# One load for wq, a pair of K tiles at the start, mirrored regions and zeros at the end, in a decode attention kernel bound by its load queue

## Chip, cores and metric

One Trainium2 chip, one core of it. The metric is the device time of one execution in microseconds (us). All runs that are compared here are of the state "fast". The profile's span leaves out some 1.9 us of each execution (381.3 us of 383.2).

## The reference

Two branches share one token x of 1024 numbers, and a sigmoid gate g mixes them:

```python
q = (x @ wq)                                   # 32 heads of 128
k, v = k_cache, v_cache                        # 4 head groups, 65536 keys each; 8 query heads share one
p = softmax(q k^T * 128**-0.5)
a = (p v) @ wo
b = (z1 * (w_sp * layernorm(z2) + b_sp)) @ w_out     # z = gelu(x @ w_in), halves z1 and z2
out = g * a + (1 - g) * b
```

162.0 MB must be read: K and V are 67.1 MB each, wq and wo 8.4 each, w_in 7.3, w_out 3.7.

## The kernel before

One buffer `kv` of five regions of 4 MB each takes every large load. A load may start once the region is no longer read. A group's K or V is four tiles of 4 MB, mostly loaded as two pairs of 8 MB. The instructions of each engine run in the order of the program.

```python
kv = big.tile([P, NKV * CT * P], BF16, name="kv")      # 5 regions of 4 MB

def load(src, shape, at):                              # at: region, may be a fraction
    ...
    ins = nc.sync.dma_start(out=v, in_=src)            # all of them on SP's queue (SPq)

win = load(win_view, (KC, F), 3)                       # regions 3 and 4
wq_t = [load(wq_view[:, i * KH:(i + 1) * KH, :], (KH, HD), 1 - i) for i in range(2)]
...                                                    # first branch, then q = x @ wq

def k_tile(g, j, kn):
    for v in range(VC):                                # four quarters
        nc.vector.transpose(...)                       # DVE, in place: L385
        while late:
            nc.vector.reduce_max(**late.pop())         # maximum of the tile before: L387
        ...                                            # 8 matmuls of 512 columns, PE: L392
    nc.scalar.copy(out=sct[g, j][:], in_=s_ps[:])
    late.append(...)

def stats(g): ...      # maximum over the group, exp on ACT, four transposes of p on DVE (L428)
def v_tile(g, j, vt): ...                              # 32 matmuls on PE: L438

build_w(0)
for j in range(NT):                                    # K of group 0: four loads
    k_tile(0, j, load_kv(A_k_cache, 0, j, (2, 1, 0, 3)[j])[0])
    if j == 1:
        build_w(1)
project(load(w_out, (FC, D), 4), FC, uT, 0, first=True)    # (view of w_out cut)
stats(0)
for g in range(1, G):
    for h in range(2):
        kn = load_kv(A_k_cache, g, 2 * h, 1 - h, 2)    # K: regions 1,2 and then 0,1
        for i in ((0, 1), (1, 0))[h]:
            k_tile(g, 2 * h + i, kn[i])
        ...
        vn = load_kv(A_v_cache, g - 1, 2 * h, 3, 2)    # V: regions 3,4
        v_tile(g - 1, 2 * h, vn[0])
        if h == 1:
            stats(g)
        v_tile(g - 1, 2 * h + 1, vn[1])
    head_out(g - 1)
...                                                    # last V, head_out, then wo in pieces of 16,8,4,2,1,1
```

## Time and profile before

| | before |
|---|---|
| time, median of 3 runs | 383.21 us (383.08 to 383.3) |
| span in the profile | 381.3 us |
| load queue's share of the DMA engines | 98.7% |
| DVE, PE busy | 57%, 60% |

From the page of the kernel before: the busy time of the engines, the share of the DMA engines and the GB/s in 40 slices of 9.5 us, and the load queue (packets, MB, share of 16 engines' time).

```profile
span 381.3 us, 2579 instructions
PE 230.5 (60%) x1372; PEld 56.4 (15%) x796; DVE 218.4 (57%) x211; ACT 39.6 (10%) x55; POOL 4.4 (1%) x10
...
DMA  9999999999999999999999999999999999999995
GB/s 385 440 433 416 423 429 440 440 485 429 407 412 419 440 442 433 433 433 440 440 428 440 440 440 440 435 434 399 419 440 435 426 440 427 426 414 433 437 412 225
...
q1 hardware_dynamic: 4180, 162.01, 98.7%
```

The queue is never short of work: only the last slice is below 9. The other engines matter where they make a load late, and after the last load.

Whether a load is late is read from the timeline of SP, which issues the loads. The columns are the start, the length of the issue itself, and what is loaded. The kernel before, 60 to 160 us:

```profile
71.80 0.33 SPq L167 DMA_DIRECT2D kv<-in_A_k_cache_dram  x1
95.92 0.33 SPq L167 DMA_DIRECT2D kv<-in_A_v_cache_dram  x1
119.11 0.33 SPq L167 DMA_DIRECT2D kv<-in_A_k_cache_dram  x1
137.00 0.33 SPq L167 DMA_DIRECT2D kv<-in_A_v_cache_dram  x1
```

The four are K of group 1 (first half), V of group 0 (first half), K of group 1 (second half) and V of group 0 (second half). The packet records in the trace tell when the queue reaches each. The packets of a load end with 16 packets of 4 bytes, as many as there are DMA engines; the first of these shows when an engine is through with the load before and turns to the next one: at 85.3, 104.7, 124.1 and 143.4 us. I call the time from the issue to that moment the *lead*: 13.5, 8.7, 4.9 and 6.4 us. In the rest of the loop it is 3.9 to 5.7 us.

What makes those loads come when they do is the work on DVE and PE. Timeline of the kernel before, some groups of instructions (start, busy us, engine, line, operation; in brackets the idle time before it and what ended it):

```profile
70.52 2.30 DVE L385 STREAM_TRANSPOSE kv<-kv 128x2048 int32<-128x2048 int32 x1
...
94.16 1.71 PE L479 MATMUL out_ps<-kv,uT 128*32 128x256 bf16 x56
...
106.90 11.09 DVE L385 STREAM_TRANSPOSE kv<-kv 128x2048 int32<-128x2048 int32 x5 [1.30 <-DMA kv<-in_A_k_cache_dram]
109.31 11.50 PE L392 MATMUL s_ps<-kv,wt 128*128 128x512 bf16 x40 [11.20 <-DVE kv L385]
```

DVE starts tile 2 of group 0 at 70.5 us without having waited. All K work of group 0 is done at 94.2, where PE goes on to w_out. At 106.9 DVE is waiting when K of group 1 lands. Its first tile is used up at 119.1, and that frees the region which the K load at 119.11 needs.

The moved bytes around that load, in stretches of 2 us (start:end, length, busy us and count of PE, PEld, DVE, ACT, POOL, then granted clock, DMA share, GB/s). A packet is counted where it starts, so single stretches jump:

```profile
122.00:124.00 2.00, 0.35 (x2) 0.10 (x1) 2.00 (x2) 0.00 (x0) 0.00 (x0) 1.00 0.38 164
124.00:126.00 2.00, 1.70 (x9) 0.29 (x3) 2.00 (x2) 0.00 (x0) 0.00 (x0) 1.00 1.21 524
126.00:128.00 2.00, 1.74 (x8) 0.38 (x4) 2.00 (x2) 0.00 (x0) 0.00 (x0) 1.00 1.06 459
128.00:130.00 2.00, 1.96 (x10) 0.40 (x5) 0.77 (x4) 0.03 (x1) 0.00 (x0) 1.00 1.14 492
```

And the end of the kernel before, from the landing of the last piece of wo:

```profile
378.86 0.41 PE L479 MATMUL out_ps<-kv,oa 128*32 128x256 bf16 x4 [0.25 <-DMA kv<-in_A_wo_dram]
...
379.31 0.37 ACT L522 CAST out_sb<-out_ps 128x256 bf16<-128x256 f32 x1 [45.27 <-PE out_ps L479]
379.71 0.33 SPq L525 DMA_DIRECT2D out_dram<-out_sb  x1
```

### The profile page before, as it was taken

The page shows a single profiled execution, that of the slowest core. Times are in us where ns is not written, and L with a number is a line of the kernel's source. Part 1 is how long each engine was busy: PE and PEld are TensorE (multiplying, and loading weights), DVE is VectorE, ACT ScalarE, POOL GpSimd, SP SyncE. Part 2 cuts the span into 40 slices and gives each one's busy share as a digit, 9 for nine tenths or more (in the row PEclk, how much of TensorE's full clock was granted, in tenths as well). Part 3 has the DMA queues.
Part 4 walks back from the last instruction along what each step waited for, and adds up shares of the span by engine and source line. Part 5 has one row for each costly group of instructions (what it writes and reads, how often), then busy time and mean ns, then how long its engine had stood idle before and what let it go on. Part 6 is the DMA issues. An engine that isn't in the chain of part 4 may idle for free.

```text
span 381.3 us, 2579 instructions
## 1 busy us (share of the span) xinstructions
PE 230.5 (60%) x1372; PEld 56.4 (15%) x796; DVE 218.4 (57%) x211; ACT 39.6 (10%) x55; POOL 4.4 (1%) x10
## 2 busy tenths in 40 slices
PE   0064467678157934796397638872976196849355
PEld 0011011112011200121011101120111011212123
DVE  4133487996687506966977059669960488560040
ACT  1001001111601100114011001040100010500000
POOL 4000000000000000000000000000000000000000
PEclk9995659998859995989589958895989579969766
DMA  9999999999999999999999999999999999999995
GB/s 385 440 433 416 423 429 440 440 485 429 407 412 419 440 442 433 433 433 440 440 428 440 440 440 440 435 434 399 419 440 435 426 440 427 426 414 433 437 412 225
DMA packets 4231, 162.17 MB, mean 425 GB/s; under 512 B 504, under 2 KB 508, under 8 KB 892
## 3 DMA queue, kind: packets, MB, share of 16 engines
q1 hardware_dynamic: 4180, 162.01, 98.7%
q8 instruction: 8, 0.13, 0.1%
q14 instruction: 3, 0.02, 0.0%
q10 hardware_dynamic: 40, 0.01, 0.0%
HBM read 162.01 MB, written 0.00 MB: 425 GB/s over the span
## 4 chain that ended last, share of the span: by engine, by line
DMA 57%; PE 24%; DVE 14%; ACT 2%; issue 1%; SPq 1%; DVEq 0%; ACTq 0%
DMA kv<-in_A_k_cache_dram 42%; PE s_ps L392 20%; DMA kv<-in_A_wo_dram 8%; DVE kv L385 8%; DMA kv<-in_A_v_cache_dram 7%; PE o_ps L438 3%; DVE pt L428 2%; DVE o_sb L452 1%; DVE mx L387 1%; ACT sc L403 1%; ACT sc L425 1%; SPq L167 1%; DVE rowt L448 1%; PE om_ps L458 0%; DVE osum L468 0%
## 5 line engine op out<-in xcount | busy, mean ns | idle before, releaser
L392 PE MATMUL s_ps<-kv,wt 128*128 128x512 bf16 x512 | 140.3, 432 | 83.8 <-DVE kv L385 83.8
L385 DVE STREAM_TRANSPOSE kv<-kv 128x2048 int32<-128x2048 int32 x64 | 142.7, 2280 | 56.3 <-DMA kv<-in_A_k_cache_dram 56.3
L438 PE MATMUL o_ps<-kv,pt 128*64 128x512 bf16 x512 | 61.8, 400 | 7.5 <-DMA kv<-in_A_v_cache_dram 7.5
L392 PEld LDWEIGHTS <-wt 128*128 128x128 bf16 x256 | 27.3, 107 | 198.1 <-issue 138.0
L403 ACT CAST sc<-s_ps 128x1024 bf16<-128x1024 f32 x16 | 16.2, 1013 | 250.0 <-PE s_ps L392 250.0
L438 PEld LDWEIGHTS <-pt 128*64 128x64 bf16 x256 | 16.1, 115 | 50.6 <-issue 48.1
L428 DVE STREAM_TRANSPOSE pt<-sc 128x1024 bf16<-128x1024 bf16 x16 | 18.6, 1217 | 6.8 <-ACT sc L425 6.8
L387 DVE TENSOR_REDUCE mx<-sc 128x1 f32<-128x1024 bf16 x12 | 14.5, 1209 | 9.3 <-ACT sc L403 9.3
L425 ACT ACTIVATE sc<-sc,nb 128x1024 bf16<-128x1024 bf16 x16 | 18.2, 1136 | 12.2 <-DVE nb L421 12.2
L448 DVE TENSOR_TENSOR rowt<-o_ps,own 128x1024 f32<-128x1024 f32 x4 | 4.8, 1194 | 24.9 <-PE o_ps L438 24.9
L458 PE MATMUL om_ps<-o_sb,hsel 128*32 128x128 f32 x8 | 2.5, 422 | 19.7 <-DVE o_sb L452 19.7
L407 DVE TENSOR_REDUCE mx<-sc 128x1 f32<-128x1024 bf16 x4 | 4.9, 1220 | 14.4 <-ACT sc L403 14.4
L278 PE MATMUL q_ps<-kv,xT 128*32 128x512 bf16 x64 | 7.2, 630 | 3.7 <-DMA kv<-in_A_wq_dram 3.7
L479 PE MATMUL out_ps<-kv,oa 128*32 128x256 bf16 x128 | 6.7, 368 | 3.6 <-DMA kv<-in_A_wo_dram 2.1
L234 PE MATMUL xb_ps<-xg,spread 8*128 8x256 bf16 x1 | 0.4, 367 | 13.2 <-DMA xg<-in_gate_w_dram 13.2
L452 DVE TENSOR_REDUCE o_sb<-rowt 128x128 f32<-128x1024 f32 x4 | 7.5, 1872 | 0.1
L345 DVE TENSOR_TENSOR rowt<-q_ps,own_b 128x512 f32<-128x512 f32 x2 | 1.3, 685 | 8.8 <-PE q_ps L278 8.8
L278 PE MATMUL z_ps<-kv,xT 128*32 128x448 bf16 x64 | 6.0, 570 | 0.0
L479 PEld LDWEIGHTS <-oa 128*32 128x32 bf16 x128 | 4.4, 124 | 6.0 <-issue 3.2
L522 ACT CAST out_sb<-out_ps 128x256 bf16<-128x256 f32 x1 | 0.4, 372 | 45.3 <-PE out_ps L479 45.3
L238 DVE TENSOR_TENSOR xm<-xb_ps,sel_i 128x128 f32<-128x128 f32 x2 | 0.5, 286 | 8.0 <-PE xb_ps L234 8.0
L278 PEld LDWEIGHTS <-xT 128*32 128x32 bf16 x64 | 2.7, 141 | 11.9 <-issue 11.9
(88 smaller groups left out, 55.5 us busy)
## 6 DMA issues: line engine op xcount, KB each, us to landing
kv<-in_A_k_cache_dram SPq DMA_DIRECT2D x4, 4096.0 KB, 46.9
kv<-in_A_wq_dram SPq DMA_DIRECT2D x2, 4096.0 KB, 33.0
kv<-in_A_v_cache_dram SPq DMA_DIRECT2D x2, 4096.0 KB
kv<-in_B_w_in_dram SPq DMA_DIRECT2D x1, 7168.0 KB
kv<-in_A_wo_dram SPq DMA_DIRECT2D x1, 4096.0 KB
kv<-in_B_w_out_dram SPq DMA_DIRECT2D x1, 3584.0 KB
kv<-in_A_wo_dram SPq DMA_DIRECT2D x1, 2048.0 KB
kv<-in_A_wo_dram SPq DMA_DIRECT2D x1, 1024.0 KB, 30.6
```

The lines of the kernel that those rows point to most:

```text
L278: ins = nc.tensor.matmul(ps[t * B:(t + 1) * B, k * HN:k * HN + n], lhsT=xT[:, i * KH + c:i * KH + c + 1].to_broadcast([P, B]), rhs=w[:, c, ...
L385: nc.vector.transpose(out=kb[:, v * n:(v + 1) * n], in_=kb[:, v * n:(v + 1) * n])
L387: nc.vector.reduce_max(**late.pop())
L392: ins = nc.tensor.matmul(s_ps[:, k * HN:(k + 1) * HN], lhsT=wt[g % 2][:, v, b].rearrange("p a v h -> p (a v h)"), rhs=kx[:, b // 2, b % 2, ...
L403: nc.scalar.copy(out=sct[g, j][:], in_=s_ps[:])
L407: nc.vector.reduce_max(**late.pop())
L425: nc.scalar.activation(out=sct[g, j][:], in_=sct[g, j][:], func=ACT.Exp, scale=SCALE, bias=nb[:, 0:1], accum_out=lss[g][:, j:j + 1])
L428: nc.vector.transpose(out=ptt[g, j][:].rearrange("p c x -> p (c x)"), in_=sct[g, j][:])
L438: ins = nc.tensor.matmul(o_ps[g][hs, e, :], lhsT=ptt[g, j][:, 2 * u:2 * u + 2, :].rearrange("p c x -> p (c x)"), rhs=vx[:, 2 * u + e], sta ...
L448: nc.vector.tensor_tensor(out=om8, in0=o_ps[g][:].rearrange("p e (v d) -> p (e v) d", d=DH), in1=own_8[:].unsqueeze(2).to_broadcast([P, 2 ...
L452: nc.vector.tensor_reduce(out=o_sb[:], in_=om8.rearrange("p x d -> p d x"), axis=AX.X, op=ALU.add)
L479: nc.tensor.matmul(out_ps[t * B:(t + 1) * B, :], lhsT=vec[:, c0 + c:c0 + c + 1].to_broadcast([P, B]), rhs=w[:, c, t * NO:(t + 1) * NO], st ...
```

## The change

The intent, as far as the diff shows it: fewer and larger loads (wq one of 8 MB for two of 4 MB; tiles 2 and 3 of group 0 one pair), and a TensorE clock kept high through the gaps at the end by multiplying operands that are mostly zeros. The pair needs two neighbouring regions, so K moves to the high regions and V to the low ones, the mirror image of before.

```diff
+WO_BUSY = {16: 4, 8: 2, 4: 1, 2: 1, 1: 0}
@@
-    wq_t = [load(wq_view[:, i * KH:(i + 1) * KH, :], (KH, HD), 1 - i) for i in range(2)]
+    wq = load(wq_view, (KC, HD), 0)
+    wq_t = [wq[:, i * KH:(i + 1) * KH, :] for i in range(2)]
@@
+    def keep_busy(n):
+        ps = pss.tile([P, 2 * HN], FP32, name="busy_ps", tag="s")
+        w = wt[G % 2][:].rearrange("p v b t u h -> p (v b t u h)")
+        for i in range(n):
+            ins = nc.tensor.matmul(ps[:, :HN], lhsT=w[:, :P], rhs=w[:, :HN], start=True, ...)
+            ...                                # the later ones keep the loaded weights
@@
-    for j in range(NT):
-        k_tile(0, j, load_kv(A_k_cache, 0, j, (2, 1, 0, 3)[j])[0])
+    for j, n, at in ((0, 1, 2), (1, 1, 3), (2, 2, 0)):
+        for i, kn in enumerate(load_kv(A_k_cache, 0, j, at, n)):
+            k_tile(0, j + i, kn)
@@
-            kn = load_kv(A_k_cache, g, 2 * h, 1 - h, 2)
-            for i in ((0, 1), (1, 0))[h]:
+            kn = load_kv(A_k_cache, g, 2 * h, 2 + h, 2)
+            for i in ((1, 0), (0, 1))[h]:
@@
-            vn = load_kv(A_v_cache, g - 1, 2 * h, 3, 2)
+            vn = load_kv(A_v_cache, g - 1, 2 * h, 0, 2)
@@
-    for j, n, at in ((0, 2, 1), (2, 1, 3), (3, 1, 4)):
+    for j, n, at in ((0, 2, 2), (2, 1, 1), (3, 1, 0)):
@@
+    keep_busy(4)
     head_out(G - 1)
+    keep_busy(4)
@@   (regions of wo mirrored as well)
             project(t, n, oa, c0, last=(c0 + n == OC))
+            keep_busy(WO_BUSY[n])
```

More of the change, by code (lines that the diff above doesn't have):

```diff
@@ L471, in head_out @@
                                 scalar2=gate[gs, :], op0=ALU.mult, op1=ALU.mult)
+    def keep_busy(n):
+        ps = pss.tile([P, 2 * HN], FP32, name="busy_ps", tag="s")
+        w = wt[G % 2][:].rearrange("p v b t u h -> p (v b t u h)")
+        for i in range(n):
+            ins = nc.tensor.matmul(ps[:, :HN], lhsT=w[:, :P], rhs=w[:, :HN], start=True,
+                                   stop=True, skip_group_check=True)
+            if i > 0:
+                same_weights(ins)
     NO = D // NB
@@ L506 @@
         head_out(g - 1)
-    for j, n, at in ((0, 2, 1), (2, 1, 3), (3, 1, 4)):
+    for j, n, at in ((0, 2, 2), (2, 1, 1), (3, 1, 0)):
         for i, vt in enumerate(load_kv(A_v_cache, G - 1, j, at, n)):
             v_tile(G - 1, j + i, vt)
+    keep_busy(4)
     head_out(G - 1)
+    keep_busy(4)
     wo_view = A_wo.rearrange("(p c) n -> p c n", c=OC)
     c0 = 0
-    for at, split in enumerate(WO_SPLIT):
+    for at, split in zip((4, 2), WO_SPLIT):
         for n in split:
```

## The prediction

> **What bounds the kernel.** The load queue: by the page's DMA part q1 takes 98.7% of 16 engines' span; 5 us stretches move 419 to 433 GB/s. The Trainium skill, "DMA: Bandwidth & Descriptors" (Specifications), puts the fabric ceiling at 435 GB/s; the trace agrees: a 64 KB packet takes 2.42 us on one of 16 engines, 433 GB/s. 162.0 MB at that rate are 374 of the span's 381.3 us. DVE (57% busy) and PE (60%) matter only where they release a region late, so that a load is issued late, and at the ends.
>
> **Slack of the loads.** Packets laid against the issues (timeline of SP): in steady state a load is issued 3.4 to 5.9 us before the first engine runs out; the last engine runs out 2.4 us later. The first load took 1.0 us from issue to packet. So 2.5 us later costs nothing, 5 us later does.
>
> **What the change does.**
> 1. wq in one load: 32 q matmuls (3.6 us) no longer run under the second half's transfer; all 64 start at 38.9 us. Weights are built at about 49.3; K tile 0 lands at 48.6: 0.7 us, absorbed, since tile 1 waits for its landing at 59.4.
> 2. K tiles 2 and 3 as a pair: tile 2 started at 70.5 us; now both land at about 78.3. From there, at 2.23 us per transpose, 1.22 per maximum: tile 3's last matmul at 101 to 102 us (94.2 before), softmax of group 0 done on DVE at 113 (105.6). K of group 1 lands at 106.9 and now waits for DVE; its first tile leaves its region 12 us later, at 125 to 126 (119.1).
>  - V's first pair is issued at about 102 (95.9), 2 us ahead of need (104.0).
>  - The next K pair is issued at 125 to 126; the queue runs dry between 123.4 and 125.8: a gap, about 1 us lost on the last engine. The next V pair (144, before 137) is just in time. DVE's 17 us of idle before the next landing absorb the delay; the lost DMA time stays.
> 3. Regions mirrored (K high, V low): the same releases in the steady state; 0.
> 4. Zeros at the end: 18 matmuls of 512 columns in PE gaps. The Trainium skill, "TensorE: Matmul & The Clock Gate" (Part 1), says the clock follows activity in windows of 3413 ns; the trace's clock records are multiples of 3.41 us. The last stretch runs at half clock: after the last landing (378.8) come 0.43 us of matmuls, a 0.37 us copy and the store. Full clock saves 0.1 to 0.2 us there. At a low clock the zeros still end before the last landing.
> 5. Two loads fewer: under 0.1 us.
>
> **Sum.** 383.2 + 1.0 - 0.15 - 0.05 = 384.0; shaded to 383.9 as the gap may close. Range 382.6 to 385.4. Chances: faster 0.01, within 2% 0.98, slower 0.01.
>
> **What would show it.** DVE idle between 70 and 78 us; first transpose of group 1 about 6 us after 106.9; a K load issued at about 125; fewer GB/s at 124 to 127 us; later landings all 1 us late; granted clock 1.0 in the last 8 us and a last matmul group of about 0.3 us.
>
> **What would make it wrong.** DVE or PE catching up sooner (no gap: 383.0), a longer issue latency (more gaps, at 102 or 144: 385.5), or zeros delaying the last projection.

## The result, and the profile after

| | before | after |
|---|---|---|
| median of 6 runs | 383.1 us (383.08 to 383.3) | 385.55 us (384.84 to 386.34) |
| ratio, 95% interval | | 1.0064 (1.0051 to 1.0077) |
| last packet of the load queue ends | 378.35 us | 380.93 us |

A ratio here is the mean time of one kernel's fast runs over that of the other's of the same rounds, so it is not quite the ratio of the medians. The change made the kernel 2.45 us slower, 0.6% and clear of the noise, though under the 2% from which a run is called slower; the forecast was +0.7, with a range that ended at 385.4. In the changed kernel the lines are shifted: L385 became L387, L392 L394, L479 L490, L167 L168.

The page after:

```profile
span 383.7 us, 2598 instructions
...
DMA  9998999999998899999999999999999999999995
GB/s 383 492 437 379 425 452 427 411 470 437 425 410 376 335 437 439 430 437 437 437 439 437 430 430 437 437 432 438 437 437 425 437 430 438 432 400 434 427 411 237
...
q1 hardware_dynamic: 3892, 162.01, 98.3%
```

The same 162.01 MB, but the slices at 115 and 125 us fell to 376 and 335 GB/s (419 and 440 before). The share of the whole span fell by only 0.4 points, which shows how little such an average tells of a single gap.

The loads after, 60 to 160 us:

```profile
71.89 0.33 SPq L168 DMA_DIRECT2D kv<-in_A_k_cache_dram  x1
102.54 0.33 SPq L168 DMA_DIRECT2D kv<-in_A_v_cache_dram  x1
125.48 0.33 SPq L168 DMA_DIRECT2D kv<-in_A_k_cache_dram  x1
144.13 0.33 SPq L168 DMA_DIRECT2D kv<-in_A_v_cache_dram  x1
```

The first is where it was; the next three are 6.6, 6.4 and 7.1 us later. Why is in the timeline of DVE and PE after:

```profile
78.82 2.31 DVE L387 STREAM_TRANSPOSE kv<-kv 128x2048 int32<-128x2048 int32 x1 [8.14 <-DMA kv<-in_A_k_cache_dram]
...
102.44 1.71 PE L490 MATMUL out_ps<-kv,uT 128*32 128x256 bf16 x56
...
113.80 11.04 DVE L387 STREAM_TRANSPOSE kv<-kv 128x2048 int32<-128x2048 int32 x5
116.17 11.02 PE L394 MATMUL s_ps<-kv,wt 128*128 128x512 bf16 x40 [9.78 <-DVE kv L387]
```

DVE waits 8.1 us for the pair. It ends K of group 0 8.3 us later. At K of group 1 it is no longer DVE that waits for the load (the bracket is gone): the landed load waits for DVE, which comes to it at 113.8 (106.9 before). The region is free at 125.5.

The stretches around that load, after:

```profile
122.00:124.00 2.00, 2.00 (x11) 0.48 (x5) 2.00 (x2) 0.00 (x0) 0.00 (x0) 1.00 0.68 295
124.00:126.00 2.00, 2.00 (x11) 0.44 (x5) 0.84 (x1) 0.51 (x1) 0.00 (x0) 1.00 0.00 0
126.00:128.00 2.00, 1.19 (x6) 0.23 (x3) 1.47 (x2) 0.50 (x1) 0.00 (x0) 1.00 1.53 524
128.00:130.00 2.00, 0.00 (x0) 0.00 (x0) 2.00 (x2) 0.00 (x0) 0.00 (x0) 1.00 1.13 492
```

From 124 to 126 us not one packet starts. By the packet records the first of the new load starts at 126.44, 0.95 us after the issue. From 165 us on every load's last packet ends 2.5 to 2.8 us later than before, to the end of the queue (2.4 to 2.9 for the small pieces of wo).

To put a number on it I used the packet records once more. A 64 KB packet takes 2.42 us in the undisturbed loop. *Idle* is the time of the 16 engines that no packet covers, *slow* the time of packets beyond their usual; both are divided by 16, and I give their sum in three windows:

| us lost (idle + slow) | before | after |
|---|---|---|
| 96 to 110 (the V load issued at 102.5) | 0.09 | 0.77 |
| 122 to 132 (the K load issued at 125.5) | 0.00 | 2.24 (1.62 idle, 0.62 slow) |
| 142 to 152 (the V load issued at 144.1) | -0.01 | 0.14 |

That is 3.1 us more than before. The rest of the span after loses 0.4 us less in total, which leaves 2.7; the mean end of the last 16 packets moved by 2.69 us, from 378.05 to 380.74. (The two agree because the same bytes are moved: this is bookkeeping, which says where the time went, not why.)

The end, after:

```profile
381.42 0.29 PE L490 MATMUL out_ps<-kv,oa 128*32 128x256 bf16 x4 [0.36 <-DMA kv<-in_A_wo_dram]
...
381.76 0.37 ACT L537 CAST out_sb<-out_ps 128x256 bf16<-128x256 f32 x1 [45.23 <-PE out_ps L490]
382.16 0.33 SPq L540 DMA_DIRECT2D out_dram<-out_sb  x1
```

The last four matmuls take 0.29 instead of 0.41 us: the zeros, or the clock, give back 0.1 us.

### The profile page after: what moved, and what is told of

It reads as the page before. It is cut to its first block, busy times and chain, and to the rows that moved or that the text cites. A ratio compares the mean times of both kernels' runs of the same rounds, so it can differ in the third digit from the quotient of the medians.

```text
span 383.7 us, 2598 instructions
## 1 busy us (share of the span) xinstructions
PE 232.9 (61%) x1388; PEld 56.0 (15%) x802; DVE 218.3 (57%) x211; ACT 39.6 (10%) x55; POOL 4.4 (1%) x10
## 3 DMA queue, kind: packets, MB, share of 16 engines
q1 hardware_dynamic: 3892, 162.01, 98.3%
HBM read 162.01 MB, written 0.00 MB: 422 GB/s over the span
## 4 chain that ended last, share of the span: by engine, by line
DMA 54%; PE 26%; DVE 15%; ACT 2%; issue 1%; SPq 0%; DVEq 0%; ACTq 0%
DMA kv<-in_A_k_cache_dram 29%; PE s_ps L394 21%; DMA kv<-in_A_wq_dram 10%; DMA kv<-in_A_wo_dram 8%; DVE kv L387 7%; DMA kv<-in_A_v_cache_dram 7%; DVE pt L430 4%; PE o_ps L440 3%; PE q_ps L280 1%; DVE mx L389 1%; ACT sc L405 1%; DVE o_sb L454 1%; ACT sc L427 1%; DVE rowt L450 1%; SPq L168 0%
## 5 line engine op out<-in xcount | busy, mean ns | idle before, releaser
L394 PE MATMUL s_ps<-kv,wt 128*128 128x512 bf16 x512 | 143.4, 441 | 81.7 <-DVE kv L387 81.7
L387 DVE STREAM_TRANSPOSE kv<-kv 128x2048 int32<-128x2048 int32 x64 | 142.6, 2279 | 58.0 <-DMA kv<-in_A_k_cache_dram 58.0
L394 PEld LDWEIGHTS <-wt 128*128 128x128 bf16 x256 | 27.7, 108 | 198.6 <-issue 135.7
L280 PE MATMUL q_ps<-kv,xT 128*32 128x512 bf16 x64 | 5.3, 501 | 7.5 <-DMA kv<-in_A_wq_dram 7.5
L490 PE MATMUL out_ps<-kv,oa 128*32 128x256 bf16 x128 | 4.6, 274 | 2.8 <-DMA kv<-in_A_wo_dram 2.4
L479 PE MATMUL busy_ps<-wt 128*128 128x512 bf16 x16 | 4.5, 383 | 0.0
```

The source lines that it names most:

```text
L280: ins = nc.tensor.matmul(ps[t * B:(t + 1) * B, k * HN:k * HN + n], lhsT=xT[:, i * KH + c:i * KH + c + 1].to_broadcast([P, B]), rhs=w[:, c, ...
L387: nc.vector.transpose(out=kb[:, v * n:(v + 1) * n], in_=kb[:, v * n:(v + 1) * n])
L394: ins = nc.tensor.matmul(s_ps[:, k * HN:(k + 1) * HN], lhsT=wt[g % 2][:, v, b].rearrange("p a v h -> p (a v h)"), rhs=kx[:, b // 2, b % 2, ...
L490: nc.tensor.matmul(out_ps[t * B:(t + 1) * B, :], lhsT=vec[:, c0 + c:c0 + c + 1].to_broadcast([P, B]), rhs=w[:, c, t * NO:(t + 1) * NO], st ...
```

## The experiments

Twelve runs were made, ten new kernels and two repeats; all gave the right result. My theory after the result: the pair alone costs the 2.5 us, and only through loads that are issued too late. The rivals: the form of the loads or the regions slow the queue; or another part of the change shares in the cost; or lateness costs only the 1.0 us that I had predicted. The table is the overview; "issued" is the second K load of group 1, and the losses are those of the three windows above.

| run | time, median | ratio (95%) | issued | lost 96-110, 122-132, 142-152 |
|---|---|---|---|---|
| before | 383.1 to 383.3 | | 119.1 | 0.1, 0.0, 0.0 |
| after | 385.55 | 1.0064 (1.0051 to 1.0077) | 125.5 | 0.8, 2.2, 0.1 |
| split23 | 383.08 | 0.9992 (0.9977 to 1.0007) | 119.2 | 0.1, 0.0, 0.0 |
| pair_only | 386.49 | 1.0086 (1.0069 to 1.0102) | 124.8 | 0.6, 2.0, 0.3 |
| delay96 | 387.04 | 1.0088 (1.0062 to 1.0114) | 125.9 | 0.1, 3.2, 0.1 |
| splitK | 385.31 | 1.0049 (1.0025 to 1.0074) | 103.8 and 124.4 | 0.2, 0.0, 1.0 |
| splitKV2 | 383.39 | 1.0003 (0.9989 to 1.0017) | 103.5 and 125.3 | 0.1, 0.0, 0.1 |
| dose2 | 383.35 | 1.0002 (0.9988 to 1.0016) | 121.1 | 0.1, 0.0, 0.0 |
| dose3 | 384.6 | 1.0038 (1.0024 to 1.0051) | 123.7 | 0.1, 1.2, 0.2 |
| before_zeros | 383.25 | 0.9997 (0.9983 to 1.001) | 118.7 | 0.0, 0.0, 0.0 |
| mirror_zeros | 383.23 | 0.9997 (0.9985 to 1.0009) | 119.1 | 0.1, 0.0, 0.0 |
| split23_again | 383.14 | 0.9995 (0.9982 to 1.0008) | 119.2 | 0.1, 0.0, 0.0 |
| wq_mirror | 383.17 | 0.9997 (0.9985 to 1.0009) | 118.9 | 0.1, 0.0, 0.0 |
| after_again | 385.48 | 1.0056 (1.0036 to 1.0077) | 126.2 | 1.3, 2.4, 0.1 |

### Undo the pair alone: split23

```diff
-    for j, n, at in ((0, 1, 2), (1, 1, 3), (2, 2, 0)):
+    for j, n, at in ((0, 1, 2), (1, 1, 3), (2, 1, 0), (3, 1, 1)):
```

> The changed kernel with K tiles 2 and 3 loaded by two loads again; wq in one load, mirrored regions and zeros stay. Gap theory (the pair alone delays the release of a K region, the queue runs dry at 124 to 126 us): K load of group 1, second half, issued at 119 to 120 us as in the kernel before, no dip, time 382.9 to 383.2 us. Rival (the mirrored regions, the single wq load or the zeros cost the 2.5 us, or most of it): 384.5 us or more.

The K load came at 119.2 us and nothing was lost: 383.08 us. All of the cost goes with the pair.

### The pair alone: pair_only

The changed kernel with these parts undone:

```diff
-    wq = load(wq_view, (KC, HD), 0)
-    wq_t = [wq[:, i * KH:(i + 1) * KH, :] for i in range(2)]
+    wq_t = [load(wq_view[:, i * KH:(i + 1) * KH, :], (KH, HD), i) for i in range(2)]
-    keep_busy(...)            # all calls
```

> The changed kernel with wq in two loads and no zeros: the pair and the regions that it needs are what is left. Gap theory: K load issued at 124 to 126 us, a dip at 124 to 128 us, time 385.0 to 386.0. Rival (part of the 2.5 us comes from wq or from the zeros; the gap costs only the 1.0 us of the prediction): 384.0 to 384.4.

The full cost is there, 386.49 us, 0.5 above the expected range. It is 0.9 above the changed kernel of another set of rounds, but the runs of these two scatter by 1.0 and 1.5 us, so I don't read the other parts' effect from that difference: whether wq or the zeros give some time back where the pair is in place stays open.

### Lateness without the pair: delay96

The kernel before, its loads untouched, with 96 matmuls whose result nobody reads:

```diff
     stats(0)
+    keep_busy(96)
     for g in range(1, G):
```

> The kernel before, all loads as they were, with 96 idle matmuls of 512 columns put on PE after the softmax of group 0, which hold back the first K tile of group 1 and so the release of its region; the result stays right. At 0.216 us each they end at about 119 us and the tile at about 126 us instead of 119. Gap theory: the K load is issued at 125 to 127 us, idle plus slow packets cost 2 to 3 us averaged over the 16 engines, time 385 to 386.5. Rival (the form of the merged loads is what slows the queue; lateness alone costs 1.0 us or less, as predicted): 383.2 to 384.2.

The timeline of PE and SP in this run, and its stretches:

```profile
98.02 20.89 PE L477 MATMUL busy_ps<-wt 128*128 128x512 bf16 x96
...
118.75 8.83 PE L392 MATMUL s_ps<-kv,wt 128*128 128x512 bf16 x40
125.88 0.33 SPq L167 DMA_DIRECT2D kv<-in_A_k_cache_dram  x1
```

```profile
122.00:124.00 2.00, 2.00 (x11) 0.48 (x5) 0.00 (x0) 0.00 (x0) 0.00 (x0) 1.00 0.38 164
124.00:126.00 2.00, 2.00 (x11) 0.47 (x5) 0.00 (x0) 0.11 (x1) 0.00 (x0) 1.00 0.00 0
126.00:128.00 2.00, 1.58 (x8) 0.29 (x4) 1.07 (x1) 0.90 (x1) 0.00 (x0) 1.00 1.46 492
128.00:130.00 2.00, 0.00 (x0) 0.00 (x0) 2.00 (x2) 0.00 (x0) 0.00 (x0) 1.00 0.30 131
```

The same empty stretch, with tiles 2 and 3 in two loads and the regions as before. This one late load cost 3.2 us of queue time (2.5 idle, 0.65 slow), a little over what I expected, and 387.04 us in all, over my range too. So a late load costs this much by itself, without the pair and the mirrored regions, and my 1.0 us was too small.

### How late is too late: dose2 and dose3

The pair is cut elsewhere: the first load holds tile 2 and a half (dose2) or three quarters (dose3) of tile 3, so tile 2 starts earlier than with the pair and later than with two loads.

```diff
+    def load_cut(j, at):
+        rows = ...                               # both tiles' rows
+        m = CT * DH * (4 + 2) // 4               # dose3: (4 + 3)
+        load(rows[:, :m], (m,), at)
+        load(rows[:, m:], (2 * CT * DH - m,), at + m / (CT * DH))
+        ...                                      # called for the pair in place of load_kv
```

> The changed kernel with the pair cut elsewhere: the first load holds tile 2 and half of tile 3, the second the rest of tile 3. Tile 2 can start when 1.5 tiles have landed, about 73.5 us (two loads: 70.5; pair: 78.8). Gap theory: the delay is 3 us less what idle time absorbs, K load of group 1 issued at 120 to 121.5 us, still over 2 us ahead of the first engine running dry (123.5): no cost, 382.9 to 383.3 us. Rival (any lateness costs in proportion to the delay): 383.9 or more, a third of the pair's cost.

> The same with three quarters of tile 3 in the first load: tile 2 can start at about 76 us. Gap theory: K load issued at 122 to 123.5 us, about as far ahead of need as a load takes from issue to first packet (1.0 us): the threshold, a small cost, 383.2 to 384.4 us. Rival (cost in proportion to the delay): 384.7 or more.

With dose2 the load came 2.0 us later than before, with a lead of 2.9 us, and nothing was lost (383.35, a hair over the range). With dose3 it came at 123.67, later than I had reckoned, with a lead of 0.3 us: 1.2 us lost there, 384.6 us, 0.2 over the range and just under the rival's bound. Against lateness in the trace (2.0, 4.6 and 6.4 us for dose2, dose3 and the pair) the window lost 0.0, 1.2 and 2.2 us. A cost in proportion to the delay would have taken 0.7 us at dose2. So the cost does not grow in proportion; it sets in below some lead. Where that is, the kept traces of all runs show together. No load with a lead of 2.9 us or more lost more than about 0.1 us. The V load of group 0's first half lost 0.2 us with a lead of 2.3 (splitK), 0.6 with 2.2 (pair_only), 0.8 with 1.9 (the changed kernel) and 1.3 with 1.2 (after_again). The second V load lost 0.1 to 0.3 with leads of 2.1 to 2.3, and 1.0 with 0.3 (splitK). The K load lost 1.2 us with a lead of 0.3 (dose3), and 2.0 to 3.2 where it was issued 0.7 to 1.8 us after the first engine had run out (pair_only, both runs of the changed kernel, delay96).

### Keep the pair, take the waits away: splitK and splitKV2

In both the pair stays, and DVE comes to K of group 1 nearly as late as in the changed kernel (113.4 and 113.1 us, against 113.8). In splitK the late K load is cut by region: the half whose region has long been free goes first.

```diff
+            if g == 1 and h == 1:
+                late_k = load_kv(A_k_cache, g, 3, 4)
+                kn = load_kv(A_k_cache, g, 2, 3) + late_k
+            else:
                 kn = load_kv(A_k_cache, g, 2 * h, 2 + h, 2)
```

> The changed kernel with everything kept, the pair too, but the K load of group 1, second half, cut in two: its tile for region 4 (free when w_out is used, 104 us) is issued first, its tile for region 3 (free at 125.5 us) second. Gap theory: the first is issued at about 104 us, the queue has 9.7 us more to do, no dip at 124 to 128 us; what is left is the nearly late V load at 102.5 us, 0.7 us: time 383.3 to 383.9. Rival (the merged pair itself slows the queue): 385 or more.

```profile
102.18 0.33 SPq L168 DMA_DIRECT2D kv<-in_A_v_cache_dram  x1
...
143.06 0.33 SPq L168 DMA_DIRECT2D kv<-in_A_v_cache_dram  x1
```

The gap at 124 us closed, as expected, but the time did not come back: 385.31 us. I had forgotten the load after it. The V load at 143.1 had been "just in time" only because the queue itself ran late; now the first engine runs out at 143.3, the V load's first packet comes at 144.0, and 1.0 us is lost there. The profiled run of this kernel, 384.15 us, fits that. The other three took 384.7 to 386.3, and their traces I do not have.

In splitKV2 the two V loads of group 0 are cut by region as well:

```diff
+            if g == 1:
+                vn = [load_kv(A_v_cache, 0, 2 * h + i, i)[0] for i in range(2)]
+            else:
                 vn = load_kv(A_v_cache, g - 1, 2 * h, 0, 2)
```

> The changed kernel with the pair and all else kept, the late K load cut in two as in splitK (which moved the gap to the V load after it: issued at 143.1 us, idle plus slow packets 1.0 us at 142 to 152), and the two V loads of group 0 cut in two by region as well, so that each part is issued when its own region is free: the second V load's first part some 3.6 us earlier, at about 139.5 us, the first V load's at about 91. Gap theory: no load late, 383.0 to 383.4 us, though the first transposes of group 1 still come at 113 us. Rival (the pair's own form, or DVE's delay, costs time apart from late loads): 384 or more.

```profile
78.64 2.31 DVE L387 STREAM_TRANSPOSE kv<-kv 128x2048 int32<-128x2048 int32 x1 [7.86 <-DMA kv<-in_A_k_cache_dram]
...
103.51 22.12 SPq L168 DMA_DIRECT2D kv<-in_A_k_cache_dram  x2
...
113.11 11.04 DVE L387 STREAM_TRANSPOSE kv<-kv 128x2048 int32<-128x2048 int32 x5
```

DVE waits for the pair and is late, but half of the K load is issued at 103.5 (the second figure of that line spans both issues). 383.39 us: no window loses more than 0.1 us, with the pair in place. With split23 and delay96 this closes the case from three sides: the pair costs nothing where no load is late, and late loads cost without the pair.

### The other parts: before_zeros, mirror_zeros, split23_again, wq_mirror, after_again

before_zeros adds the zeros alone to the kernel before. mirror_zeros is split23 with wq in two loads, wq_mirror is split23 without the zeros; their edits are those of pair_only. The last four ran on one chip.

> The kernel before with the zeros at the end alone. Theory: granted clock 1.0 in the last 8 us, the last four matmuls 0.3 instead of 0.41 us, so 0.1 to 0.15 us less: 383.0 to 383.2 where the kernel before has 383.1 to 383.3 on the same chip. Rival (the zeros delay the projection or do nothing): same or up to 0.4 us more.

> The changed kernel with wq in two loads and tiles 2 and 3 in two loads: the mirrored regions and the zeros are what is left. Theory: K load of group 1 issued at 119 us, no gap, 383.0 to 383.3 us, as the kernel before less 0.1 for the clock at the end. Rival (the mirrored regions cost time by themselves): 383.6 or more.

> split23 once more (the change without the pair), now beside mirror_zeros on one chip: the difference of the two is the single wq load. Theory: q ready 2 us later is absorbed before tile 1 lands, so within 0.15 us of mirror_zeros, 383.0 to 383.3. Rival (the single wq load costs): 0.3 us or more above it.

> split23 without the zeros: the difference from split23_again is the zeros. Theory: granted clock 0.5 at the end in most runs, first of the last matmuls to the store 0.1 us longer; time 0.0 to 0.2 us above split23_again. Rival (no effect or harm): 0.1 us or more below it.

> The changed kernel once more, beside the three others on one chip. Theory: the gap again, K load issued at 125 to 126 us, 384.8 to 386.4 us, 2 to 3 us above split23_again, and a wider scatter of its runs than of theirs, since how late the load is depends on when the clock of the matmuls before it rises. Rival (the 2.5 us were of the first chip): below 384.

The regions (mirror_zeros, 383.23 with the zeros), the single wq load (383.14 against 383.23) and the zeros (383.14 against 383.17; and 383.25 against 383.21 for before_zeros) are each within 0.1 us of nothing. In before_zeros the last four matmuls took 0.29 us and the store was issued 0.11 us sooner after the last landing, as expected, but its last landing was 0.3 us later than in the profile of before, and the total does not show the gain. In wq_mirror the last four took 0.29 us without any zeros: there the clock was up by itself. Over all the profiles, the last four took 0.29 us in each of the ten with zeros; of the four without, they took 0.41 in two (before, pair_only) and 0.29 in two (delay96, wq_mirror). So the zeros save 0.1 us where the clock would be low, which is not measurable in the time.

after_again confirms the loss beside three kernels without it on one chip, 385.48 us, and the scatter (384.32 to 386.73, while the runs of each of the other three stay within 0.55 us). Its profiled run took 386.39 us, with the V load at 103.26 and the K load at 126.16, each 0.7 us later than in the 385.58 us profile, and its windows lost 0.6 us more. The phase of the clock, which I had expected to make the lateness vary, is not what differs there: the 0.8 us is there when the pair lands (tile 2 starts at 79.61, not 78.82), and the first tile of group 1 then takes 11.7 us from its first transpose to the K load in both. In pair_only it takes 11.1 us, and there the granted clock goes from 0.5 to 1.0 at 119.4 instead of 120.6 us. So both can play a part, and these three profiles do not settle what the scatter of the runs comes from. Nor does the time follow the issue alone: pair_only's K load came 0.7 us sooner than the changed kernel's, and its profiled run took 386.3 us.

No version beats the kernel before clearly: the best, split23, had 0.9992 and 0.9995, with 1 inside both intervals.

## Why the prediction was wrong

- **What bounds the kernel**: right. So was the use of the Trainium skill, "DMA: Bandwidth & Descriptors" (Specifications, 435 GB/s): the undisturbed loads ran at 433 in both kernels.
- **wq**: right in what it cost. q's matmuls began at 38.8 us and took 5.3, tile 1's first transpose came at 59.5 as before (59.45), and split23_again against mirror_zeros shows no cost. The prediction had tile 0 wait 0.7 us for the weights; it waited for its own landing and started at 49.7 us (48.6 before).
- **The pair's delay**: right to within 1 us at every stage: tile 2 at 78.8 (predicted 78.3), w_out reached at 102.4 (101 to 102), softmax done at 113.9 (113), the V load at 102.5 (102), the K load at 125.5 (125 to 126), the next V load at 144.1 (144).
- **The size of the gap: the step that failed.** The prediction said "a gap, about 1 us lost on the last engine". It was 2.24 us. Two errors are in it. First, I charged only the engine that ran dry last (126.2 us). The engines ran dry between 124.2 and 126.2 and all restarted at 126.4 to 126.8, so the last one was idle for 0.2 us, but all of them for 1.6 us on average, and it was the average that came through: the last packet of this load ended 2.6 us later than before (147.99 against 145.36). Restarted within 0.4 us of each other, the engines ended this load 1.8 us apart again. Why stays open. Second, I let the queue resume at full speed. The first packet of each engine took 2.9 to 3.3 us instead of 2.42, another 0.6 us. delay96, with no other load late, lost 3.2 us to one load that came at 125.9.
- **The V load at 102: wrong.** The prediction said "2 us ahead of need (104.0)" and counted that as free. The lead was indeed 1.9 us (102.54 to 104.49), but that was not enough: 0.77 us lost. Why a load that comes 1.9 us ahead still costs, when the K load's first packet followed its issue by 0.95 us, stays open. splitKV2, which issues half of it at 91 us, lost 0.1. The slack that I stated, "2.5 us later costs nothing, 5 us later does", held in the doses (2.0 us later 0, 4.6 us later 1.2).
- **The sum**: the terms are 0.7 for the V load (0.77, less the 0.09 lost there before) and 2.24 for the K load where I had 0 and 1.0. That is 1.9 us, against a miss of 1.65 us (385.55 against 383.9); the other differences are 0.15 us more lost at the V load of 144 and 0.4 us less in the rest of the span. Under "what would make it wrong" the prediction had named 385.5 for gaps at 102 or 144 too. The number fits by luck: it blamed a longer issue latency, and the latency was 0.95 us, no longer than assumed.
- **The zeros**: right in mechanism and size (0.1 us, granted clock 1.0 from 366 us on); the Trainium skill, "TensorE: Matmul & The Clock Gate" (Part 1), has the clock follow activity in windows of 3413 ns, and the trace's clock records agree (3.41 us and multiples). But wq_mirror shows that the clock can be up without them, so the gain depends on the run.

The Trainium skill's "DMA: Bandwidth & Descriptors" (Rules for kernel authors) says to issue a DMA early and wait on its semaphore late, and to coalesce many small transfers. The second is meant for transfers under 64 KB, and no run here tests it. Loads of 4 MB are far above that, and merging two of them made things worse: the first tile of the 8 MB load was not touched before the whole load had landed (last packet at 78.3, first transpose at 78.8 us), and undoing the merge (split23) restored the time.

## What to carry to other kernels

In a kernel bound by its load queue, list for every load when it is issued and when the queue reaches it; a change that delays a release is free while that lead stays at some 2.9 us or more here, and below that it must be charged. Charge a late load with the mean idle time of all DMA engines plus a slow restart, not with the wait of the last engine, and look at the loads after it, for mending one can uncover the next. Merging two loads delays the first half's work by the second half's transfer, so do it only where the consumer has time to spare.

## What the Trainium skill lacked or had wrong

- "DMA: Bandwidth & Descriptors" (Specifications) gives about 0.6 us to the first byte for loads from SP, and does not say from where it counts. Here the first packets came 1.02 us after the start of the first issuing instruction and 0.95 us after the one at 125.48, when engines stood idle; from the end of these instructions (0.40 and 0.33 us long) it was 0.62 us in both, so the figure agrees if it is counted from there.
- No page that I read tells what a queue costs when it resumes: the first 64 KB packet of each engine took 2.9 to 3.5 us instead of 2.42 (0.6 to 0.7 us in after, delay96 and dose3), and some packets were slow even where a load came before the queue ran out (0.5 us at the V load with a lead of 1.9 us).
- "DMA: Bandwidth & Descriptors" (Rules for kernel authors) advises to coalesce small transfers, under 64 KB; it doesn't say that a merged load holds back its first half's consumer. Here that was 8.1 us of DVE idle time and 2.45 us in all.
- No page that I read has the spread of the engines within one load queue. In the kernel before, the first and the last engine ended a load 0.4 us apart in the first loads, 1.6 from 57 us on and 1.8 to 2.2 in the loop.
